# Superblocks of 480 columns in the second layer of an attention and two-layer MLP kernel

## The chip, the cores and the metric

The kernel runs on one core of a Trainium2 chip. The metric is the device time of one execution in microseconds: before the change 1749.05, the median of three runs between 1747.64 and 1750.35. The profile is one further execution with its own time.

## What is computed

Attention inside chunks of 64 tokens over q, k and v of shape (8, 8, 576, 64), and then two gated MLPs over the 4608 tokens, the second behind a normalization:

```python
attn_out = softmax(scale * q_c @ k_c.T) @ v_c          # by chunks of 64
x = attn_out.transpose(0, 2, 1, 3).reshape(4608, 512)
# first layer
g = x @ w_gate; h = g * sigmoid(g) * (x @ w_val)       # 512 -> 1536
x = h @ w_out                                          # 1536 -> 512
# second layer
xn = x / sqrt(mean(x * x) + 1e-6) * rms_g
g = xn @ w_gate2; h = g * sigmoid(g) * (xn @ w_val2)
out = h @ w_out2
```

All is float32. The kernel makes a product exact enough by splitting each operand into a high and a low part: one logical matmul is three on TensorE (`mm3`, lines 633 to 636).

## The kernel before

The tokens are cut into 36 tiles of 128. Eight of them are taken out of their order and put at the end: `last` (line 319), so that `home` says which tile stands at a position and `order` the reverse. A stretch of positions is therefore not always a stretch of rows of the output.

**First layer.** The first 28 positions make seven blocks of 512 tokens. They run as plain triple matmuls (`emit_g`, `emit_v`, `emit_y`), with the attention of later tiles, the conversion of the weights and the normalization of finished blocks spread between them on a list of positions. Each tile's attention result is split into `xh` and `xl` of its block, or, for the eight last tiles, stored to `x1_d` (`att_hi`, `att_lo`).

**Superblocks.** From line 1531 on the work goes by superblocks of two halves of equal width `tw` (`SB`, lines 904 to 909). Superblock 0 is the first layer for the eight last tiles (2 x 512 tokens); superblocks 1 to 5 are the second layer. A superblock uses a scheme of seven products in place of eight for 2 x 2 blocks. It has two stages:

- gate and value: for each of 6 chunks (`fp`) 14 products (7 for g, 7 for v, in the order of `GV`), each of 6 matmuls `tw` columns wide with one weight tile of 256 KB (`gv_mm`). After each one, `gv_after` takes the bank out on ScalarE (a copy, `snap`) and VectorE (sum, sigmoid, product).
- y: 42 items in pairs, in the order of `ORDER` for k and then `fp`, each of 2 x 3 matmuls (`y_mm`), fed by `h_prep`, which casts h on ScalarE and subtracts on VectorE, 8 items ahead. Behind the fifth of each six, `y_after` finishes a quarter. The output positions come in the order 11, 22, 21, 12 (the second digit is the half), after items 11, 29, 35 and 41; each is made of two pieces, q 0 and 1.

Weights stand in a ring of 16 tiles. `load_ring(wn + 16)` after each product, or each pair of items, issues the DMAs of those tiles whose place has come free, all on SP's queue. In the y stage the first tiles of the next superblock's gate products come in the same way, two behind each pair. SP issues in program order and waits at each instruction for what it needs.

**Output.** `y_out` adds and transposes a piece on VectorE into the tile `yo` (there are two, used in turn) and writes it with one DMA per 32 partitions and per run of contiguous output rows, `rows(t0 + j * tw, tw)`, on SP's queue (line 1180; in the last superblock some go on ScalarE's queue). In the last but one superblock the DMAs are held in a list, which `flush` issues during the last one. `x_load` and `x_prep` bring and split the next superblock's input in the y stage. In superblock 1 VectorE, ScalarE and GpSimd also run the normalization of the eight last tiles and the conversion of two chunks of weights, from the tables `late` and `norm`.

Of the kernel before, what the change touches and what calls it, by code (L numbers as in the profile page):

```python
# [19 lines left out]
def tile_kernel(  # L20
# [23 lines left out]
    P = 128  # L44
# [133 lines left out]
    def chunk(j, f):  # L178
        return f if j % 2 == 0 else NF - 1 - f
# [136 lines left out]

    NCH = NT // CH
    SC = S // CH
    last = [32, 33, 13, 34, 35, 21, 22, 23]
    home = [i for i in range(NT // P) if i not in last] + last  # L320
    order = [home.index(i) for i in range(NT // P)]

    def rows(t, n):
        runs = []
        for a in range(0, n, P):
            i = home[(t + a) // P]
            if runs and home[(t + a) // P - 1] == i - 1:
                runs[-1][1] += P
            else:
                runs.append([a, P, i * P])  # L330
        return runs

    EARLY = NW // P + 1
# [477 lines left out]
    def score_at(i):  # L811
        return NP + 7 * (i - 8)

    for i in range(NW // P, NT_):
        j = order[i] * P // NW
        if i >= 8:
            a = score_at(i)
# [66 lines left out]
    for j, p, nm in w1_at:  # L884
        a = 3 * min(chunk(j, 2 * p), chunk(j, 2 * p + 1)) + (3 if nm == "o" else 0)
# [17 lines left out]
    YTAG = {"g": {"A": "y2", "D": "a0", "C": "y0"}, "v": {"A": "y3", "D": "a1", "C": "y1"}}  # L903
    SB = [(TAIL, NW)]
    t0 = 0
    for tw in (512, 512, 512, 384, 384):
        SB.append((t0, tw))
        t0 += 2 * tw
    assert t0 == NT
# [245 lines left out]
    def y_out(s, q, pos, src, n):  # L1155
        nonlocal nout
        t0, tw = SB[s]
        m = "gv"[q]
        slow = s == len(SB) - 2 and pos != "11"
        if n:  # L1160
            tag = ("ysb0", "ysb1")[q] if slow and pos == "12" else ("acc", "sq")[nout % 2]
            shape = [P, 2, 512] if tag in ("ysb0", "ysb1") else [P, 512]
            t = st.tile(shape, F32, tag=tag, name=f"yt{q}{pos}_{s}")
            t = t[:, 0] if len(shape) == 3 else t
            nc.vector.tensor_add(t[:, :tw], src[:, :tw], snaps[m, n][:, :tw])
            src = t
        tag = ("acc", "sq")[nout % 2] if slow and pos == "21" else ("ah", "al")[nout % 2]
        o = st.tile([P, 512], F32, tag=tag, name=f"yo{q}{pos}_{s}")
        nout += 1
        nc.vector.transpose(out=o[:, :tw], in_=src[:, :tw])  # L1170
        i, j = int(pos[0]) - 1, int(pos[1]) - 1
        r0, c0 = t0 + j * tw, i * HK + q * P
        for a, (x, n, r) in [(a, run) for a in range(0, P, 32) for run in rows(r0, tw)]:
            dst = out[r:r + n, c0 + a:c0 + a + 32].rearrange("(b t) d -> t b d", t=32)
            src_ = o[a:a + 32, x:x + n].rearrange("t (b d) -> t b d", d=32)
            queue = nc.scalar if s == len(SB) - 1 and pos in ("12", "21") and a >= 64 else nc.sync
            if s == len(SB) - 2:
                held.append((dst, src_))
            else:
                queue.dma_start(out=dst, in_=src_)  # L1180
# [460 lines left out]
```

## Time and profile before

| | before |
|---|---|
| median of the runs | 1749.05 us |
| lowest, highest | 1747.64, 1750.35 us |
| profiled execution | 1741.64 us |
| its span | 1739.8 us |
| mean granted TensorE clock | 0.999 |
| TensorE busy | 1715.2 us, 99% |
| VectorE, ScalarE, GpSimd busy | 1271.6, 812.6, 543.9 us |

The span runs from the first to the last instruction. Times inside the trace are counted from its start. Matmul records overlap, since matmuls are pipelined; how fast they follow each other is read from their starts. "SPq" is SP's queue of DMA issues, DVE is VectorE, ACT ScalarE, POOL GpSimd, PE TensorE, PEld its weight loads. A bracket at the end of a timeline row is the idle time ahead of it and what ended that.

### The profile page before, as it was taken

The numbers are of one execution on the slowest core, as the hardware profiler recorded it, in microseconds if no ns is written. First come the engines' busy times: TensorE is split into PE (matmuls) and PEld (weight loads), VectorE is DVE, ScalarE is ACT, GpSimd is POOL, SyncE is SP. The second block draws the span as 40 slices with busy tenths as digits, with TensorE's granted clock in tenths as the row PEclk, the third lists the DMA queues.
The fourth block names the chain that finished last, engine by engine and source line by source line (L and its number), as shares of the span: only waits on it lengthen the run. The fifth ranks groups of instructions, "written<-read, shape, count | busy, mean of one in ns | idle before, by whom it ended". The sixth has DMA issues, their size and how long they took to land.

```text
span 1739.8 us, 29450 instructions
## 1 busy us (share of the span) xinstructions
PE 1715.2 (99%) x9978; PEld 1445.9 (83%) x9978; DVE 1271.6 (73%) x2232; ACT 812.6 (47%) x1902; POOL 543.9 (31%) x527
## 2 busy tenths in 40 slices
PE   7999999999999999999999999999999999999998
PEld 5788888888888888877877888888888888999998
DVE  6996777777678776467899678954885488569566
ACT  6773444445444444335556444532453354345343
POOL 1003546455555735334544632100210011002000
PEclk9999999999999999999999999999999999999999
DMA  9995878867786775856755797787678758989986
GB/s 233 332 248 147 229 199 218 238 172 211 216 209 209 194 228 192 289 166 226 243 173 176 224 317 233 207 257 217 180 206 266 211 170 245 301 267 273 285 253 175
DMA packets 462789, 392.86 MB, mean 226 GB/s; under 512 B 278832, under 2 KB 334896, under 8 KB 462640
## 3 DMA queue, kind: packets, MB, share of 16 engines
q1 hardware_dynamic: 423760, 311.68, 61.6%
q10 hardware_dynamic: 38880, 79.31, 14.4%
q8 instruction: 80, 1.31, 0.3%
q14 instruction: 69, 0.57, 0.1%
HBM read 310.90 MB, written 79.95 MB: 225 GB/s over the span
## 4 chain that ended last, share of the span: by engine, by line
PE 84%; DVE 7%; DMA 4%; ACT 2%; issue 1%; SPq 1%; POOL 0%; ACTq 0%; DVEq 0%; POOLq 0%
PE g L634 4%; PE g L635 4%; PE v L634 4%; PE g L636 4%; PE v L635 4%; PE v L636 4%; PE y L634 2%; PE y L635 2%; PE y L636 2%; PE y_b L635 2%; PE y_b L634 2%; PE y_b L636 2%; PE ygA L634 1%; PE ygA L635 1%; PE yvA L635 1%
## 5 line engine op out<-in xcount | busy, mean ns | idle before, releaser
L1094 POOL TENSOR_TENSOR h<-h,h 128x512 f32<-128x512 f32 (+1 forms) x36 | 46.6, 1294 | 506.0 <-DVE h L1072 499.6
L1130 DVE TENSOR_TENSOR hp<-h,hp 128x512 fp32r<-128x512 f32 (+1 forms) x216 | 147.4, 710 | 6.0 <-ACT hp L1129 5.9
L1052 ACT ACTIVATE sig<-sgt 128x512 f32<-128x512 f32 (+1 forms) x108 | 64.6, 598 | 186.8 <-DVE sgt L1060 186.7
L544 DVE STREAM_TRANSPOSE pT<-p 32x128 f32<-32x128 f32 x448 | 135.5, 303 | 17.9 <-POOL p L528 11.7
L1129 ACT CAST hp<-h 128x512 fp32r<-128x512 f32 (+1 forms) x216 | 121.3, 584 | 50.1 <-PE yvA L636 18.9
L1053 DVE TENSOR_TENSOR sgt<-sgt,sig 128x512 f32<-128x512 f32 (+1 forms) x108 | 77.0, 713 | 89.7 <-ACT sig L1052 89.7
L991 POOL TENSOR_TENSOR xf<-xf,xf 128x512 f32<-128x512 f32 (+1 forms) x48 | 81.7, 1702 | 170.8 <-DVE xo0l L987 75.0
L634 PE MATMUL g<-xh,wg 128*128 128x512 f32 x336 | 132.9, 395 | 2.1 <-ACT xh L608 1.1
L634 PE MATMUL v<-xh,wv 128*128 128x512 f32 x336 | 132.8, 395 | 1.7 <-DVE sg L663 1.0
L635 PE MATMUL g<-xl,wg 128*128 128x512 f32 x336 | 131.0, 390 | 0.4 <-DVE xl L628 0.4
L636 PE MATMUL g<-xh,l 128*128 128x512 f32 x336 | 131.0, 390 | 0.0
L636 PE MATMUL v<-xh,l 128*128 128x512 f32 x336 | 131.0, 390 | 0.0
L635 PE MATMUL v<-xl,wv 128*128 128x512 f32 x336 | 130.9, 390 | 0.0
L666 ACT CAST hh<-sg 128x512 fp32r<-128x512 f32 x84 | 52.1, 620 | 134.8 <-DVE sg L663 119.5
L646 ACT ACTIVATE sg<-g 128x512 f32<-128x512 f32 x84 | 50.1, 597 | 113.9 <-PE g L636 111.2
L528 POOL TENSOR_TENSOR p<-p,r 128x512 f32<-128x512 f32 x36 | 40.2, 1117 | 188.5 <-DVE r L527 131.7
L668 DVE TENSOR_TENSOR hl<-sg,hh 128x512 fp32r<-128x512 f32 x84 | 72.8, 866 | 35.2 <-ACT hh L666 34.5
L647 DVE SCALAR_TENSOR_TENSOR sg<-sg,g 128x512 f32<-128x512 f32 x84 | 57.3, 683 | 54.3 <-ACT sg L646 53.8
L1072 DVE TENSOR_TENSOR h<-h,sgt 128x512 f32<-128x512 f32 (+1 forms) x108 | 74.8, 693 | 3.7
L634 PEld LDWEIGHTS g<-xh,wg 128*128 128x128 f32 x336 | 63.0, 188 | 17.3 <-DVE sg L647 1.6
L634 PEld LDWEIGHTS v<-xh,wv 128*128 128x128 f32 x336 | 63.1, 188 | 16.4 <-DVE sg L663 2.0
L636 PEld LDWEIGHTS g<-xh,l 128*128 128x128 f32 x336 | 63.1, 188 | 13.7 <-DVE l L175 0.4
(855 smaller groups left out, 5254.4 us busy)
## 6 DMA issues: line engine op xcount, KB each, us to landing
wrg<-w_scratch SPq DMA_DIRECT2D x210, 256.0 KB, 3.5
wrv<-w_scratch SPq DMA_DIRECT2D x210, 256.0 KB, 3.5
wro<-w_scratch SPq DMA_DIRECT2D x210, 256.0 KB, 3.2
l<-lo_scratch ACTq DMA_DIRECT2D x51, 512.0 KB, 4.4
lo<-lo_scratch ACTq DMA_DIRECT2D x58, 256.0 KB, 4.8
w_scratch<-wsg ACTq DMA_DIRECT2D x18, 512.0 KB, 4.4
w_scratch<-wsv ACTq DMA_DIRECT2D x18, 512.0 KB, 4.1
xv<-in_v_dram SPq DMA_DIRECT2D x136, 64.0 KB, 4.3
```

Of the source, the lines that this page charges most:

```text
L544: nc.vector.transpose(out=pT[o:o + 32, :, r:r + 32], in_=pt[r:r + 32, :, z, b * 32:b * 32 + 32])
L634: nc.tensor.matmul(o, sh, mh, start=first, stop=False, skip_group_check=free)
L635: nc.tensor.matmul(o, sh, ml, start=False, stop=False, skip_group_check=free)
L636: nc.tensor.matmul(o, sl, mh, start=False, stop=last, skip_group_check=free)
L647: return sg, lambda: nc.vector.scalar_tensor_tensor(out=sg[:, :n], in0=sg[:, :n], scalar=1.0, in1=g[:, :n], op0=ALU.add, op1=ALU.mult)
L668: return product, lambda: nc.vector.tensor_sub(hl[:, :n], sg[:, :n], hh[:, :n].bitcast(F32))
L991: nc.gpsimd.tensor_sub(o, a, b)
L1052: nc.scalar.activation(sg[:, :tw], src[:, :tw], AF.Sigmoid)
L1053: nc.vector.tensor_mul(t[:, :tw], src[:, :tw], sg[:, :tw])
L1072: nc.vector.tensor_mul(h[:, :tw], src[:, :tw], sgt[pos][:, :tw])
L1129: nc.scalar.copy(hh[:, :tw], src)
L1130: nc.vector.tensor_sub(hl[:, :tw], src, hh[:, :tw].bitcast(F32))
```

## The change

The second layer's superblocks get the half widths 480, 480, 480, 480 and 384 in place of 512, 512, 512, 384 and 384. Their borders then no longer fall on tiles of 128 tokens, so `rows` works out the runs of output rows token by token: it walks to the end of a tile or of the stretch, whichever is nearer, and joins a piece to the run before it if the output rows follow on. The list of the eight tail tiles is changed: tile 16 takes the place of 13, and the order is 32, 33, 34, 35, 16, 21, 22, 23.

```diff
-    last = [32, 33, 13, 34, 35, 21, 22, 23]
+    last = [32, 33, 34, 35, 16, 21, 22, 23]
     home = [i for i in range(NT // P) if i not in last] + last
     order = [home.index(i) for i in range(NT // P)]
 
     def rows(t, n):
         runs = []
-        for a in range(0, n, P):
-            i = home[(t + a) // P]
-            if runs and home[(t + a) // P - 1] == i - 1:
-                runs[-1][1] += P
+        a = 0
+        while a < n:
+            i, p = home[(t + a) // P], (t + a) % P
+            step = min(P - p, n - a)
+            if runs and runs[-1][2] + runs[-1][1] == i * P + p:
+                runs[-1][1] += step
             else:
-                runs.append([a, P, i * P])
+                runs.append([a, step, i * P + p])
+            a += step
         return runs
...
     SB = [(TAIL, NW)]
     t0 = 0
-    for tw in (512, 512, 512, 384, 384):
+    for tw in (480, 480, 480, 480, 384):
         SB.append((t0, tw))
         t0 += 2 * tw
     assert t0 == NT
```

## Rows read from the trace of the kernel before

**Rows 1.** the page, part 1: busy time, share of the span, instructions of each engine

```profile
PE 1715.2 (99%) x9978; PEld 1445.9 (83%) x9978; DVE 1271.6 (73%) x2232; ACT 812.6 (47%) x1902; POOL 543.9 (31%) x527
```

**Rows 2.** superblocks 1 to 5: us, busy (x) PE PEld DVE ACT POOL, clock, DMA, GB/s

```profile
954.20:1127.60 173.40, 173.16 (x762) 142.39 (x761) 137.26 (x194) 82.75 (x150) 64.64 (x54) 1.00 0.78 247
1127.60:1299.20 171.60, 171.60 (x758) 141.82 (x757) 116.38 (x172) 70.25 (x122) 22.27 (x14) 1.00 0.72 214
1299.20:1471.10 171.90, 171.67 (x758) 141.84 (x757) 112.53 (x173) 68.32 (x122) 19.32 (x14) 1.00 0.75 220
1471.10:1603.00 131.90, 131.35 (x758) 130.98 (x757) 92.12 (x173) 56.74 (x122) 17.06 (x14) 1.00 0.89 280
1603.00:1733.80 130.80, 130.80 (x756) 130.80 (x755) 81.68 (x159) 51.60 (x108) 6.32 (x6) 1.00 0.82 245
```

**Rows 3.** timeline, TensorE: start, us, line, tiles; first and last matmuls of stages

```profile
1127.59 0.39 PE L634 MATMUL p0gA<-xo0h,wrg 128*128 128x512 f32 x1
...
1241.83 0.39 PE L634 MATMUL ygA<-hp,wro 128*128 128x512 f32 x1
...
1299.18 0.39 PE L634 MATMUL p0gA<-xo0h,wrg 128*128 128x512 f32 x1
...
1602.97 0.33 PE L634 MATMUL p0gA<-xo0h,wrg 128*128 128x384 f32 x1
...
1733.84 0.34 PE L636 MATMUL yvC<-hp,wro 128*128 128x384 f32 x1
```

**Rows 4.** timeline, TensorE, around product 14 of superblock 3

```profile
1317.99 0.39 PE L636 MATMUL p0vC<-xo6h,wrv 128*128 128x512 f32 x1
1318.61 0.47 PE L634 MATMUL p1gA<-xo0h,wrg 128*128 128x512 f32 x1 [0.23 <-DMA wrg<-w_scratch]
1318.92 0.39 PE L635 MATMUL p1gA<-xo0l,wrg 128*128 128x512 f32 x1
```

**Rows 5.** timeline, TensorE, stalls in superblocks 1 and 4

```profile
1014.31 0.50 PE L634 MATMUL p3vA<-xo0h,wrv 128*128 128x512 f32 x1 [0.24 <-DVE h L1072]
...
1578.04 0.44 PE L635 MATMUL ygC<-hp,wro 128*128 128x384 f32 x1 [0.55 <-DVE hp L1130]
```

**Rows 6.** timeline, SP's queue: issues of superblock 2's y stage and after, in order

```profile
1264.71 4.38 SPq L1180 DMA_DIRECT2D out_dram<-yo  x8
...
1274.65 6.88 SPq L928 DMA_DIRECT2D wro<-w_scratch  x10
...
1282.57 0.32 SPq L928 DMA_DIRECT2D wrv<-w_scratch  x1
1286.62 7.79 SPq L1180 DMA_DIRECT2D out_dram<-yo  x16
...
1297.39 6.03 SPq L1180 DMA_DIRECT2D out_dram<-yo  x8
...
1306.43 9.12 SPq L1180 DMA_DIRECT2D out_dram<-yo  x16
1315.65 0.41 SPq L928 DMA_DIRECT2D wrg<-w_scratch  x1
```

**Rows 7.** timeline, SP's queue: last two pieces of superblock 1

```profile
1125.13 4.17 SPq L1180 DMA_DIRECT2D out_dram<-yo  x8
...
1132.31 6.96 SPq L1180 DMA_DIRECT2D out_dram<-yo  x8
```

**Rows 8.** timeline, VectorE, at the start of superblock 3

```profile
1303.65 0.71 DVE L1170 STREAM_TRANSPOSE yo<-yt 128x512 f32<-128x512 f32 x1 [4.94 <-DMA out_dram<-yo]
```

**Rows 9.** stretches, early in the kernel (columns as in rows 2)

```profile
18.80:22.20 3.40, 3.40 (x72) 2.95 (x71) 2.94 (x7) 2.30 (x4) 1.92 (x2) 0.50 0.78 222
```

**Rows 10.** timeline, TensorE, just ahead of that stretch

```profile
15.74 0.69 PE L474 MATMUL s<-kT,qT 64*64 64x64 f32 x32 [1.52 <-ACT kT L440]
...
18.66 1.00 PE L552 MATMUL tp<-ident,p 128*128 128x128 f32 x4 [1.63 <-POOL p L528]
```

**Rows 11.** timeline, SP's queue: piece 22 of superblock 3

```profile
1456.43 4.17 SPq L1180 DMA_DIRECT2D out_dram<-yo  x8
```

## Prediction

> **What bounds the kernel now.** I read the page first: TensorE is busy in 99% of the span [rows 1]. The table of stretches, cut at the five superblocks of the second layer, says that this holds there too: 173.4, 171.6, 171.9, 131.9 and 130.8 us long, with TensorE busy for all but a few tenths of a microsecond in each, at full clock [rows 2]. VectorE (62 to 79% busy there) and the DMA engines (0.72 to 0.89) have room left on the average. So only two things can move the time: the pace of the matmuls, and stalls of TensorE. As every matmul record overlaps its neighbour, I take the pace from starts, not from durations.
>
> **Pace of the matmuls.** A superblock has 756 matmuls: 6 chunks x 14 products x 6, then 42 x 6, whatever its width. At 512 columns 504 of them start between 1127.59 and 1241.83 us: 114.24 / 504 = 226.67 ns each. At 384 columns the last superblock has 755 starts after its first between 1602.97 and 1733.84: 130.87 / 755 = 173.34 ns [rows 3]. The difference, 53.33 ns, is 128 columns at 2.4 GHz exactly; both are columns/2.4 + 13.3 ns. A matmul of 480 columns is not in the trace. Its bounds are its neighbours', 173.34 and 226.67; I take the line through both, 213.33 ns, because nothing but columns separates them. Then three superblocks at 226.67 and two at 173.34 make 1026.7 ns for one matmul of each, and four at 213.33 and one at 173.34 make 1026.7 too. The widths alone change nothing: 756 x 0. What is on VectorE, ScalarE and GpSimd keeps its number of operations and its columns and lies beside TensorE, as before.
>
> **Stalls that exist.** There is little to win. At the start of superblock 3 the first matmul of product 14 (p1gA) starts 0.62 us after the one before it where 0.23 is the pace, and the next one 0.08 late; the row names the DMA of its weight tile [rows 4]. That is 0.5 us. In the y stage the product ygC waits for VectorE's split of h, worst in superblock 4, where TensorE is idle for 0.55 us and the starts lose 0.8; by the same timeline it is about 0.2 in superblocks 1 and 2, none in 3 and 5. In the first superblock 0.5 us more is lost at p3vA, behind VectorE, which runs the tail's normalization in between [rows 5].
>
> **The runs of output rows.** Here the change adds something. An output piece goes out in 4 DMAs for each run of contiguous rows, for two quarters, so a position costs SP 8 issues per run. Before, only superblock 2 has a half with two runs (tiles 12 | 14, 15, 16), and the last one has one (13 | 34, 35). After: superblocks 1, 2 and 4 have one run in each half, superblock 3 has two in both (row tokens 1920 to 2047 | 2176 to 2527, and 2528 to 2687 | 3072 to 3391, since 16 and 21 to 23 are now missing from the order), the last one still two and one. Superblock 2 gives back 16 issues, superblock 3 gets 32 more.
>
> SP issues them in program order, and the ring's weight tiles stand behind them. Product 14 of the next superblock is the first whose weights are issued after the last output piece: 14 are already in the ring. Follow superblock 2 into 3 [rows 6], times against its end at 1299.18 [rows 3]: piece 22 (16 issues) from -12.56, in 7.79 us; six weight tiles, 2.9 to 3.0; piece 21 (8 issues) 6.03; six tiles; piece 12 (16 issues) 9.12; the weights of product 14 at +16.47. Its first matmul starts 2.96 us after the issue [rows 4, 6], at 19.43, where 14 products x 6 x 226.67 ns allow 19.04. This is the 0.4 us stall, and SP never waits for TensorE between 22 and 12. Superblock 1, with 8 issues everywhere, has ended piece 12 at 1139.3 (1132.31 + 6.96), +11.7 against its end at 1127.59 [rows 3, 7]: 4 us earlier than needed, with the 2.96.
>
> Small pieces cost SP as much as large ones: sixteen issues of half the mean size took 7.79 us, 0.49 each, when little else was queued. The Trainium skill (DMA: Bandwidth & Descriptors, Issuing engines are not separate DMA queues) calls the time to initiate a DMA "usually small relative to the DMA itself", and its section on the anatomy of a DMA gives about 50 ns of dispatch, for another path; by that, sixteen issues would be an estimated 0.8 us and superblock 3 would stall nothing. The rows speak against it for this queue.
>
> Now superblock 3 after the change, at 213.33 ns, against its end. Piece 22 can go out when VectorE has transposed it. Before, in superblock 2, that was 5.1 us after the quarter's last matmul (16.3 + 1.4 - 12.56); 15/16 of it is 4.8, so -15.36 - 1.28 + 4.8 = -11.8. Sixteen issues with their gap, 7.9: -3.9. Six tiles, 2.9: -1.0. Piece 21 now has 16 issues, behind six weight tiles as piece 12 was in superblock 2, so 9.2: +8.2. Six tiles, 2.9: 11.1. Piece 12, 9.2: 20.3. Issue to matmul, 2.96: 23.2. Allowed are 14 x 6 x 213.33 = 17.9. **Stall: 5.3 us.** Lower bound: both pieces at the quiet 7.9, which takes 2.6 off: 2.7. Upper: piece 11 has 16 issues as well, and the loads behind it (4 of x, then tiles at 0.69 us) may not be through at -11.8; they ended 3.7 us before piece 22 in superblock 2 [rows 6], piece 11 adds 3.5 (7.9 for 4.4), and the shorter pace takes 1 to 2 more: up to 1 us, 6.3. VectorE is also held longer: it is first in, first out, and piece 12's transposes waited 4.9 us for piece 21's DMAs to leave their tile [rows 8]. That hold will last until about +11 instead of +7, and the work behind it then reaches the banks of products 12 to 14 about as they are needed. It lies beside the SP stall, and adds nothing while that is the longer.
>
> **The clock.** TensorE has no such gap now. Near the start it did sparse small matmuls with gaps of 1.5 and 1.6 us, and the granted clock was 0.50 (1.2 GHz) in the following 3.4 us [rows 9, 10]. After a gap of 5 us the same can happen; a stretch of 3.4 us at half pace costs 1.7. Bounds 0 and 1.7; no row is of a single long gap, so I take the middle, 0.85.
>
> **Small terms.** The 0.5 us before superblock 3 go (its predecessor has 8 issues per piece now, and has 3 us to spare at 480: 11.8 + 3.0 against 17.9). The ygC stalls, one quarter of the way from 0.2 to 0.8, make 4 x 0.36 = 1.4 instead of 1.2: +0.2 (between -0.8 and +0.6). The first superblock's fixed work is pressed into 1/16 less time: +0.2 (0 to 0.8). Held pieces of the second last superblock keep 32 issues, which the last one's products still cover. Attention: tile 13 goes to block 3 and 16 to the tail, the same operations, both two blocks ahead of need: 0. The end: the last superblock keeps width, runs and queues: 0. Sum: 5.3 - 0.5 + 0.2 + 0.2 + 0.85 = **+6.0 us**. The profiled execution took 1741.6 us (span 1739.8) and would take 1747.6; it ran 7 us under the median of the runs, to which I add the same 6.0: **1755.0**.
>
> **Rivals.**
> (a) Not slower: VectorE reaches piece 22 earlier. Superblock 3 itself, with its 384-wide successor, had piece 22 out at 1456.43, 14.6 us ahead of its end at 1471.1 and so 3.1 us after the quarter's end instead of 5.1 [rows 2, 11]; it speaks against this that the successor is 480 wide now. With that and all pieces at 7.9 us, the tile goes out at 15.9 and arrives at 18.9: a stall of 0.9, and without a dip of the clock +0.8, 1749.9. It decides when product 14's tile is issued before +18.6, where the stall falls under 3.6.
> (b) SP's time in those issues is waiting on bytes, not on issues, and more pieces of the same bytes cost nothing. For it: eight large issues took between 4.2 and 7.0 us [rows 6, 7], so queued bytes do hold SP. Against it: sixteen took 7.79 for as many bytes as eight in 4.17. No stall then: -0.5 + 0.4, 1749.0. The Trainium skill's sentence above would have it so.
> (c) The matmul of 480 columns doesn't lie on the line. Rounded up to the price of 512 it costs 4 x 756 x 13.3 ns = 40 us, 1795; without the fixed 13.3 ns it gains 40, 1715. The exact 53.33 speaks against both. To be faster by 0.2% it would have to lie 3.1 ns under the line.
>
> **How the numbers follow.** 0.2% (3.5 us) is about what a measurement of this kernel tells from no change. Forecast 0.65, between 1751.3 (stall 2.7, nothing else) and 1758 (6.3 and every upper end); (a) 0.22; (b) 0.05; (c) 0.03 slower and 0.05 faster. The forecast's own low end is within 0.2%, the upper part of (a) with a clock dip is not: these balance. Slower 0.68, same 0.27, faster 0.05. Range 1748.5 to 1759.5: it holds the forecast, (b) by a little and most of (a), and leaves out (c) and the rest, under 2 in 10.
>
> **What would show it.** In the profile after: starts 213.3 ns apart at 480 columns; three rows of sixteen output issues on SP around the end of superblock 3, and one gap of TensorE of some 5 us at p1gA of superblock 4, released by the DMA of wrg; no such gap at superblock 3. A second stretch of half clock right behind it decides the clock term. Wrong it is if that gap is under 3 us, if another pace is seen, or if TensorE stalls at other superblocks' starts.

## The result, and the profile after

The changed kernel takes 1764.3 us (median of 5 runs, 1762.52 to 1766.7) where the kernel before takes 1748.06 (5 runs, 1747.49 to 1750.35): ratio 1.0088, 95% interval 1.0074 to 1.0102. It is slower by 16 us, as forecast in direction; the forecast was 6 us, and its range ended at 1759.5. The profiled execution of after took 1764.37 us, its span 1762.6.

The stretches of after, cut at the first matmul of each superblock of the second layer as those of before [rows 2] (columns: us, then busy time and count of PE, PEld, DVE, ACT, POOL, then the granted clock, the DMA share and GB/s), and a short one 24.7 us into superblock 4:

```profile
959.10:1124.60 165.50, 165.21 (x762) 142.39 (x761) 130.05 (x194) 79.36 (x150) 62.56 (x53) 1.00 0.81 257
1124.60:1288.40 163.80, 163.80 (x758) 141.90 (x757) 110.17 (x172) 66.61 (x122) 20.96 (x14) 1.00 0.77 227
1288.40:1454.00 165.60, 164.00 (x757) 141.79 (x756) 109.93 (x172) 66.61 (x122) 20.23 (x14) 1.00 0.73 217
1454.00:1624.90 170.90, 165.86 (x757) 142.99 (x757) 107.06 (x173) 65.36 (x122) 18.68 (x14) 0.99 0.78 230
1624.90:1755.80 130.90, 130.90 (x756) 130.87 (x756) 81.75 (x159) 51.68 (x108) 6.33 (x6) 1.00 0.82 241
1478.70:1482.00 3.30, 3.30 (x10) 2.75 (x9) 0.00 (x0) 0.56 (x1) 0.00 (x0) 0.50 0.98 349
```

Read it against a clean superblock. Superblock 2 has no idle time at all and takes 163.80 us, which is 756 matmuls at 216.67 ns. The line of the prediction gave 213.33. So the first thing to see is that even the undisturbed superblock is 2.5 us longer than forecast. Superblocks 3 and 4 add 1.8 and 7.1 us of their own; superblock 5 is what it was.

The sum from the starts of the matmuls: the five superblocks took 779.62 us before (954.2 to 1733.8) and take 796.75 now, 17.1 more. Work at pace, with 171.36 us for 756 matmuls at 512 columns and 131.05 at 384, was 3 x 171.36 + 2 x 131.05 = 776.2 and is 4 x 163.80 + 131.05 = 786.25: **10.1 us of pace**. What each superblock lost beyond it went from 2.0, 0.2, 0.5, 0.85 and 0 us to 1.7, 0, 1.8, 7.1 and 0: **7.0 us of stalls**. Together they are the 16.2 us between the medians, to within the spread of the runs. The profile of after also reaches superblock 1 some 5 us later than that of before (959.1 and 954.2); the experiment "The kernel before once more" shows that this is not the change.

The timeline of TensorE gives both (start, us, line, tiles; the bracket is the idle time before and what ended it):

```profile
1124.55 0.38 PE L637 MATMUL p0gA<-xo0h,wrg 128*128 128x480 f32 x1
...
1233.75 0.38 PE L637 MATMUL ygA<-hp,wro 128*128 128x480 f32 x1
...
1438.33 0.48 PE L637 MATMUL ygA<-hp,wro 128*128 128x480 f32 x1 [1.60 <-ACT s3g L1047]
...
1466.44 0.48 PE L637 MATMUL p0gA<-xo5h,wrg 128*128 128x480 f32 x1 [1.85 <-ACT s2g L1047]
...
1474.13 0.38 PE L639 MATMUL p0vC<-xo6h,wrv 128*128 128x480 f32 x1
1477.70 0.45 PE L637 MATMUL p1gA<-xo0h,wrg 128*128 128x480 f32 x1 [3.19 <-DMA wrg<-w_scratch]
...
1479.03 0.60 PE L639 MATMUL p1gA<-xo0h,wrg 128*128 128x480 f32 x1
1479.43 0.60 PE L637 MATMUL p1vA<-xo0h,wrv 128*128 128x480 f32 x1
```

The first two rows have 504 matmuls between them: 109.20 / 504 = 216.67 ns each, against 226.67 at 512 and 173.34 at 384 [rows 3]. The 3.19 us at p1gA is the forecast gap, behind the forecast DMA: product 14 (products are counted from 0) starts 23.67 us after superblock 4's start at 1454.03. Ahead of it TensorE is already idle for 1.85 us at p0gA, and for 1.60 in superblock 3 at ygA, which was not forecast. Counted by the starts, which come a little later still behind a gap, p1gA loses 3.4 us, p0gA 2.1 and ygA 1.8. From 1478.64 on matmuls start 0.40 us apart, 480 columns at 1.2 GHz, while the stretch above shows a clock of 0.50.

SP's queue around the end of superblock 3 (x16 is the number of issues in the row), which answers to [rows 6]:

```profile
1419.14 7.72 SPq L1183 DMA_DIRECT2D out_dram<-yo  x16
1426.96 2.79 SPq L931 DMA_DIRECT2D wro<-w_scratch  x6
1429.85 2.13 SPq L970 DMA_DIRECT2D xf<-xn_scratch  x4
...
1441.53 8.86 SPq L1183 DMA_DIRECT2D out_dram<-yo  x16
...
1454.37 8.17 SPq L1183 DMA_DIRECT2D out_dram<-yo  x16
...
1465.52 9.07 SPq L1183 DMA_DIRECT2D out_dram<-yo  x16
1474.69 0.40 SPq L931 DMA_DIRECT2D wrg<-w_scratch  x1
```

Four pieces (11, 22, 21, 12) of sixteen issues each. From 1441.53 to 1474.69 SP is issuing nearly all the time; the tile that product 14 wants goes out 20.66 us after the superblock's start (20.3 forecast), and its matmul starts 3.01 us later.

### The profile page after: what moved, and what is told of

The parts are those of the page before. It is cut to its first block, busy times and chain, and to the rows that moved or that the text cites. A ratio compares the mean times of both kernels' runs of the same rounds, so it can differ in the third digit from the quotient of the medians.

```text
span 1762.6 us, 29464 instructions
## 1 busy us (share of the span) xinstructions
PE 1727.8 (98%) x9978; PEld 1459.4 (83%) x9978; DVE 1271.6 (72%) x2232; ACT 813.5 (46%) x1902; POOL 543.0 (31%) x527
## 4 chain that ended last, share of the span: by engine, by line
PE 84%; DMA 5%; DVE 5%; SPq 2%; ACT 1%; issue 1%; POOL 1%; ACTq 0%; DVEq 0%; POOLq 0%
PE g L637 4%; PE g L638 4%; PE g L639 4%; PE v L637 4%; PE v L639 4%; PE v L638 4%; PE y L637 2%; PE y L639 2%; PE y L638 2%; PE y_b L637 2%; PE y_b L639 2%; PE y_b L638 2%; PE ygA L637 1%; PE ygA L639 1%; PE ygA L638 1%; PE yvA L638 1%
## 5 line engine op out<-in xcount | busy, mean ns | idle before, releaser
L1097 POOL TENSOR_TENSOR h<-h,h 128x480 f32<-128x480 f32 (+2 forms) x36 | 46.6, 1295 | 524.0 <-DVE h L1075 517.6
L1055 ACT ACTIVATE sig<-sgt 128x480 f32<-128x480 f32 (+2 forms) x108 | 64.5, 598 | 189.9 <-DVE sgt L1063 189.7
L1133 DVE TENSOR_TENSOR hp<-h,hp 128x480 fp32r<-128x480 f32 (+2 forms) x216 | 146.1, 703 | 6.2 <-ACT hp L1132 6.1
L547 DVE STREAM_TRANSPOSE pT<-p 32x128 f32<-32x128 f32 x448 | 135.6, 303 | 16.3 <-POOL p L531 10.0
L1132 ACT CAST hp<-h 128x480 fp32r<-128x480 f32 (+2 forms) x216 | 121.4, 584 | 50.0 <-PE yvA L639 23.3
L1056 DVE TENSOR_TENSOR sgt<-sgt,sig 128x480 f32<-128x480 f32 (+2 forms) x108 | 76.9, 712 | 90.4 <-ACT sig L1055 90.4
L994 POOL TENSOR_TENSOR xf<-xf,xf 128x480 f32<-128x480 f32 (+2 forms) x48 | 81.0, 1687 | 172.1 <-DVE xo0l L990 122.4
L1075 DVE TENSOR_TENSOR h<-h,sgt 128x480 f32<-128x480 f32 (+2 forms) x108 | 74.4, 689 | 3.7
L666 DVE SCALAR_TENSOR_TENSOR sg<-v,sg 128x512 f32<-128x512 f32 x84 | 57.6, 686 | 26.0 <-PE v L639 24.8
```

The source lines that it names most:

```text
L547: nc.vector.transpose(out=pT[o:o + 32, :, r:r + 32], in_=pt[r:r + 32, :, z, b * 32:b * 32 + 32])
L666: nc.vector.scalar_tensor_tensor(out=sg[:, :n], in0=vv[:, :n], scalar=0.5, in1=sg[:, :n], op0=ALU.mult, op1=ALU.mult)
L994: nc.gpsimd.tensor_sub(o, a, b)
L1055: nc.scalar.activation(sg[:, :tw], src[:, :tw], AF.Sigmoid)
L1056: nc.vector.tensor_mul(t[:, :tw], src[:, :tw], sg[:, :tw])
L1075: nc.vector.tensor_mul(h[:, :tw], src[:, :tw], sgt[pos][:, :tw])
```

## The experiments

**Widths put back, order and runs alone.** The changed kernel with the old widths.

```
-    for tw in (480, 480, 480, 480, 384):
+    for tw in (512, 512, 512, 384, 384):
```

> The new tail order and the new rows, with the old widths 512, 512, 512, 384, 384. Theory: of the 16 us, about 10 come from the pace of the 480-column matmuls and 8 to 9 from the stalls around superblock 3 and 4 that its 64 output issues make; the order and the rows alone cost nothing. Here all halves of superblocks 1 to 4 are one run, so also the 0.5 us stall at superblock 3 goes: 1747 to 1749 us, ratio 0.999 to 1.001. Rival: the order of the tail tiles itself disturbs the first layer (the gap of 4.0 us at the ssq matmul and its half-clock stretch): then 5 us over the kernel before, ratio 1.003.

Measured: 1747.43 us (10 runs) against 1747.39 (13 runs), ratio 0.9998 (0.9989 to 1.0008). With these widths each half of superblocks 1 to 4 is one run. The gap at product 14 of superblock 3 [rows 4] is gone:

```profile
1304.64 0.39 PE L637 MATMUL p0gA<-xo0h,wrg 128*128 128x512 f32 x1
...
1323.45 0.39 PE L639 MATMUL p0vC<-xo6h,wrv 128*128 128x512 f32 x1
1323.68 0.39 PE L637 MATMUL p1gA<-xo0h,wrg 128*128 128x512 f32 x1
...
1476.00 0.33 PE L637 MATMUL p0gA<-xo0h,wrg 128*128 128x384 f32 x1
```

Product 14 starts 0.23 us after its predecessor, and the superblock takes 171.36 us, exactly the pace. So other tail tiles and the new way to work out the runs cost nothing, and the half microsecond that they win is too small to be measured. The whole loss comes with the widths.

**Five widths in one kernel.** The same line, to read the pace of each width.

```
+    for tw in (512, 480, 448, 448, 416):
```

> Half widths 512, 480, 448, 448, 416: a look at the pace of each width in the stretches without a stall. Theory A (on the line columns/2.4 + 13.3 ns where the width is a multiple of 64 columns, 3.3 ns above it otherwise): 226.7, 216.7, 200.0, 200.0, 190.0 ns. Theory B (the same with multiples of 128): 448 columns take 203.3 ns too. Theory C (13/12 of columns/2.4, with 512 the exception): 448 take 202.2 and 416 take 187.8 ns. Rival: the excess has nothing to do with the width but with what else runs then: 448 and 416 lie anywhere between 198 and 206 and between 185 and 193, and the single starts scatter.

Measured from starts: 512 columns 226.75 ns, 480 216.66 (755 starts), 448 202.67 (612 starts from 1297.55 to 1421.58, and 202.66 in the next superblock), 416 188.34 (755 starts). One run took 1767.41 us.

```profile
1133.75 0.38 PE L637 MATMUL p0gA<-xo0h,wrg 128*128 128x480 f32 x1
...
1297.33 0.38 PE L639 MATMUL yvC<-hp,wro 128*128 128x480 f32 x1
1297.55 0.36 PE L637 MATMUL p0gA<-xo0h,wrg 128*128 128x448 f32 x1
...
1421.58 0.36 PE L637 MATMUL ygC<-hp,wro 128*128 128x448 f32 x1
```

The 216.7 ns belong to the width of 480, wherever the superblock stands and whatever its runs are. Over columns / 2.4 GHz the four widths stand 13.4, 16.7, 16.0 and 15.0 ns. None of the three rules of the expectation (200.0, 203.3 or 202.2 at 448; 190.0, 190.0 or 187.8 at 416) gives all of them. Against the rival, that the excess comes from what else runs, stand the two superblocks at 448: they agree to 0.01 ns.

**The old tail tiles with the new widths.** This moves issues from superblock 3 to superblock 2: both then have 48.

```
-    last = [32, 33, 34, 35, 16, 21, 22, 23]
+    last = [32, 33, 13, 34, 35, 21, 22, 23]
```

> Widths 480, 480, 480, 480, 384 and new rows, with the old order of the tail tiles. Superblocks 2 and 3 then have one half of one run and one of two: 48 issues each in place of 32 and 64. Theory: the pace stays at 216.7 ns (10.1 us); each of the two boundaries behind them stalls at p1gA by 1 to 2 us, without a half-clock stretch and without the gaps at ygA and p0gA: 5 to 6 us less than the changed kernel, 1758 to 1760 us, ratio 1.006. Rival (the stalls come from the width and not from the number of issues): the gaps at ygA, p0gA and p1gA of 2.0, 2.2 and 3.6 us stay, 1764 us.

Measured: 1759.62 us (4 runs), ratio 1.0066 (1.0049 to 1.0083). The gaps moved with the issues; there is now one at product 14 of superblock 3 and one of superblock 4, a little larger than expected, none at ygA or p0gA, and no half clock:

```profile
1310.92 0.45 PE L637 MATMUL p1gA<-xo0h,wrg 128*128 128x480 f32 x1 [2.61 <-DMA wrg<-w_scratch]
...
1476.64 0.45 PE L637 MATMUL p1gA<-xo0h,wrg 128*128 128x480 f32 x1 [1.67 <-DMA wrg<-w_scratch]
```

**Half of superblock 3's output DMAs left out.** Its pieces then have 8 issues each, as before the change, and half its output columns are not written.

```
         for a, (x, n, r) in [...]:
+            if s == 3 and a >= 64:
+                continue
```

> The changed kernel, with superblock 3 leaving out half of its output DMAs (the 32-partition groups 64 and 96), so that it issues 32 and not 64; half of its output columns are not written. Theory: SP's chain is 8 x 0.49 us shorter per piece position; the gaps at ygA, p0gA and p1gA and the half-clock stretch go, 8 to 9 us: 1755 to 1757 us, ratio 1.004 to 1.005. What stays is the pace, 10 us. Rival (VectorE's and ScalarE's work at 480 columns makes the gaps): they stay, 1764 us.

Measured: 1755.49 us (4 runs), ratio 1.0045 (1.003 to 1.006): 8.8 us less than after, which is what superblocks 3 and 4 lost beyond their pace (1.8 + 7.1). Both now take 163.80 us. SP's pieces and product 14 of superblock 4:

```profile
1419.25 3.78 SPq L1185 DMA_DIRECT2D out_dram<-yo  x8
...
1439.96 3.95 SPq L1185 DMA_DIRECT2D out_dram<-yo  x8
...
1449.53 4.30 SPq L1185 DMA_DIRECT2D out_dram<-yo  x8
...
1456.80 4.96 SPq L1185 DMA_DIRECT2D out_dram<-yo  x8
```

```profile
1470.26 0.38 PE L639 MATMUL p0vC<-xo6h,wrv 128*128 128x480 f32 x1
1470.47 0.38 PE L637 MATMUL p1gA<-xo0h,wrg 128*128 128x480 f32 x1
```

What stays, 8.1 us, is the pace (10.1) less the small stalls that are gone (about 2). The run takes away bytes with the issues, so it doesn't tell them apart; the next one does.

**The kernel before, with superblock 1's runs cut in two.** Same bytes, same rows, 512 columns; only the number of issues of superblock 1 doubles, to 64.

```
+    def split2(runs):
+        return [h for a, n, r in runs for h in ([a, P, r], [a + P, n - P, r + P])]
...
-        for a, (x, n, r) in [(a, run) for a in range(0, P, 32) for run in rows(r0, tw)]:
+        for a, (x, n, r) in [(a, run) for a in range(0, P, 32) for run in (split2(rows(r0, tw)) if s == 1 else rows(r0, tw))]:
```

> The kernel before (widths 512), with the output runs of superblock 1 cut in two by hand, so that it issues 64 DMAs and not 32; the same bytes go to the same rows. The pace of the matmuls is untouched. Theory (SP's issues at 0.49 us each hold the weights behind them): with the sum of the prediction at 226.67 ns, piece 22 at -12.6 and then 7.9, 2.9, 9.2, 2.9, 9.2 and 2.96 us, the matmul of product 14 comes at +22.5 where 19.0 are allowed: gaps of 3.4 us in all at p0gA and p1gA of superblock 2, with or without a half-clock stretch (up to 1.7): 1750.5 to 1753 us, ratio 1.002 to 1.003. Rival (more pieces of the same bytes cost SP nothing, and the gaps need 480 columns): 1747.5 us, ratio 1.000.

Measured: 1757.02 us (4 runs) against 1748.3, ratio 1.0044 (1.0029 to 1.0059); more than expected. SP's issues, and product 14:

```profile
1121.28 9.61 SPq L1183 DMA_DIRECT2D out_dram<-yo  x16
...
1133.87 9.11 SPq L1183 DMA_DIRECT2D out_dram<-yo  x16
...
1145.96 9.64 SPq L1183 DMA_DIRECT2D out_dram<-yo  x16
```

```profile
1158.78 0.76 PE L637 MATMUL p1gA<-xo0h,wrg 128*128 128x512 f32 x1 [3.26 <-DMA wrg<-w_scratch]
```

In the kernel before the last two of these pieces were issued in 4.17 and 6.96 us [rows 7]. Product 14 starts 23.58 us after the superblock's start at 1135.20, with the gap at the same matmul as in after. So more issues of the same bytes are enough to make the gap, without the width of 480 and without the new tail. The 8.7 us are, by the starts, 1.3 at ygA, 1.1 at p0gA, 3.4 at p1gA, about 1.4 for half clock (0.50 from 1158.3 to 1161.6), and 1.5 more at the product 14 of superblock 3 (its first matmul was 0.4 and 0.6 us late in two profiles of the kernel before, 2.1 here). Superblock 2, whose issues delay that product, has no more of them than before; whether its longer gap comes from the cut or from this execution is not shown.

**The pace at eighteen widths.** In the kernel before, four of the seven products (k = 4, 5, 2 and 6) of g and of v in each superblock stream only part of their columns, and the rest of those products is not computed; the one with k = 6 uses 64 stationary columns instead of 128 in superblocks 1 and 3.

```
+    SWEEP = {1: {4: (32, 480, P), 5: (0, 480, P), 2: (64, 448, P), 6: (0, 480, 64)}, ...}
...
+        a, n, q = SWEEP.get(s, {}).get(k, (0, tw, P))
-            c = slice(kt * P, (kt + 1) * P)
+            c = slice(kt * P, kt * P + q)
-                o, w[:, 0, c], w[:, 1, c], xh[:, kt, :tw], xl[:, kt, :tw],
+                o[:q, a:a + n], w[:, 0, c], w[:, 1, c], xh[:, kt, a:a + n], xl[:, kt, a:a + n],
```

> The kernel before, where the gate and value products k = 4, 5, 2 and 6 of each superblock stream only a part of the columns (the rest of those products is not computed): 464, 448, 432, 416 in superblock 2; 496, 504, 400 in 3; 368 to 320 in 4; 304 to 256 in 5; in superblock 1 columns 32 to 511 and 0 to 479 and 64 to 511; and 480 and 512 columns with a stationary operand of 64 columns. A look at the pace of each. Theory (the width decides, and only multiples of 128 columns come as cheap as columns/2.4 + 13.3 ns): 480 takes 216.7 wherever it begins; 448 takes 203.3, 416 188.3; 496, 464 and 432 lie 15 to 17 ns over columns/2.4; 256 takes 120 ns unless the weight loads hold it at some 173. Rival A (the place of the first column decides): 480 from column 32 takes another time than from 0. Rival B (the weight load decides): with 64 stationary columns 480 comes down to the line, 213.3, or lower, and 512 too.

Measured, as the mean distance of some 66 starts inside runs of twelve equal matmuls (ns), and what of it is over columns / 2.4. Single distances more than some 12% above the middle one are left out as stalls: twelve at 272 columns, four at 256 (119.98 ns with them), two at 480 with 64 stationary columns:

| columns | pace | over | columns | pace | over | columns | pace | over |
|---|---|---|---|---|---|---|---|---|
| 512 | 226.67 | 13.3 | 416 | 188.73 | 15.4 | 320 | 146.55 | 13.2 |
| 504 | 226.91 | 16.9 | 400 | 181.05 | 14.4 | 304 | 137.68 | 11.0 |
| 496 | 220.0 | 13.3 | 384 | 173.36 | 13.3 | 288 | 131.67 | 11.7 |
| 480 | 216.36 | 16.4 | 368 | 166.74 | 13.4 | 272 | 125.26 | 11.9 |
| 464 | 209.64 | 16.3 | 352 | 160.55 | 13.9 | 256 | 119.0 | 12.3 |
| 448 | 202.36 | 15.7 | 336 | 153.74 | 13.7 | | | |
| 432 | 196.18 | 16.2 | | | | | | |

With 64 stationary columns 480 took 219.36 and 512 took 230.3, not less, though each weight load took 0.13 to 0.14 us in place of 0.19. A start at column 32 or 64 didn't help either (218.03 at 480 in the disturbed superblock 1, 202.27 at 448). So 480 is on the upper side of a band of 11 to 17 ns, and both anchors of my line, 512 and 384, happened to lie at 13.3. That only multiples of 128 are cheap is refuted (496, 320 to 368). The length of the weight load is not it either. What sets the step is left open.

**The kernel before once more.** No edit; this is to see whether the first layer changed.

> The kernel before, one more profile. The profile of the changed kernel has a gap of 4.0 us at the first-layer matmul ssq (block 1) and a half-clock stretch behind it, 5 us in all, ahead of everything that the change touches; the profiled execution of the kernel before has not, and is itself 4 us faster than any timed run of it. Theory: the gap belongs to most executions of either kernel: block 1 takes 109 to 112 us here too (106.4 in the profile of before), and the whole 1745 to 1749. Rival: it comes with the change: block 1 takes 106.4 us again.

Measured: 1749.41 us, span 1747.6. After shows an idle gap of 4 us in the first layer that the first profile of before doesn't have. The second one has it too, behind the same engine. The matmul ssq in the first profile of before, in this one, and in after:

```profile
190.40 0.50 PE L742 MATMUL ssq<-ah,ones 128*128 128x512 f32 x1 [0.15 <-ACT p L500]
```

```profile
194.90 0.80 PE L742 MATMUL ssq<-ah,ones 128*128 128x512 f32 x1 [3.88 <-ACT p L500]
```

```profile
193.63 0.80 PE L745 MATMUL ssq<-ah,ones 128*128 128x512 f32 x1 [3.99 <-ACT p L503]
```

and in this run the clock behind it:

```profile
193.30:200.00 6.70, 5.10 (x12) 4.05 (x13) 4.71 (x12) 6.06 (x18) 3.60 (x5) 0.50 0.73 173
```

That block takes 111.7 us in both this run and after, 106.4 in the first profile. The gap stands in every other profile of this document too, of either kernel, with 3.4 to 4.0 us. So it is no effect of the change: the profile that the prediction was made from, 1741.64 us, was of the one execution without this stall, 4 us under the fastest timed run of the kernel before (1745.79). In superblocks 1 to 5, after minus this run is 17.0 us, as with the first profile.

**Half of two pieces on ScalarE's queue.** In after, pieces 21 and 12 of superblock 3 issue half their DMAs on ScalarE, as the last superblock does.

```
-            queue = nc.scalar if s == len(SB) - 1 and pos in ("12", "21") and a >= 64 else nc.sync
+            queue = nc.scalar if s in (3, len(SB) - 1) and pos in ("12", "21") and a >= 64 else nc.sync
```

> The changed kernel, with half of the DMAs of superblock 3's pieces 21 and 12 (partition groups 64 and 96) issued on ScalarE's queue, as in the last superblock. Theory: SP issues 8 and 8 there in place of 16 and 16, so product 14's weights come 7 to 8 us earlier; the gap at p1gA (3.6 us) and the half-clock stretch (1.6) go, that at p0gA (2.2) shrinks: 1757 to 1760 us, ratio 1.006. The gap at ygA (2.0), which lies ahead of these pieces, stays. Rival (ScalarE, which then waits for the transposes in its own queue, delays its copies of the banks by as much): 1762 to 1766 us.

Measured: 1769.05 us (4 runs), ratio 1.011 (1.0092 to 1.0129), 5 us worse than after. The gap at p1gA is gone, but a larger one stands ahead of it:

```profile
1471.83 0.77 PE L637 MATMUL p0gA<-xo4h,wrg 128*128 128x480 f32 x1 [7.80 <-ACT s1g L1047]
```

```profile
1453.14 5.87 ACTq L1183 DMA_DIRECT2D out_dram<-yo  x8
...
1465.24 5.93 ACTq L1183 DMA_DIRECT2D out_dram<-yo  x8
1471.21 0.56 ACT L1047 COPY s1g<-p0gA 128x480 f32<-128x480 f32 x1 [11.57 <-DMA out_dram<-yo]
```

The rival of the expectation came out, worse than its number. ScalarE empties the PSUM banks that the next products need; its copy of p0gA came 11.6 us after the instruction before it, 5.6 of them until the second piece's first issue and 5.9 in its issues. The gap at ygA stayed, as expected (2.2 us idle).

**The load of x ahead of piece 11.** In after, the load of superblock 4's x that stood behind piece 11's sixteen issues is moved ahead of them.

```
+                if n == 10 and s == 3:
+                    x_load(s + 1, 1)
+                    xnext = x_prep(s + 1, 1)
...
-                if n == 16 and s + 1 < len(SB):
+                if n == 16 and s + 1 < len(SB) and s != 3:
```

> The changed kernel, with the second half of superblock 4's input (four DMAs, x_load) put on SP's queue before piece 11 of superblock 3 and not 6 items after it. A look. Theory for the gap at ygA (2.0 us): the loads stand behind the 16 issues of piece 11, land late, and ScalarE waits 2.8 us for them with its copy of the bank (s3g) behind the waiting cast. Then the gap at ygA is under 0.3 us here, and the gaps at p0gA and p1gA stay at 5 to 6 us in all. Rival: the gap comes from VectorE's work at 480 columns (the split of h ahead of it): it stays at 1.8 to 2.0 us.

Measured: 1764.07 us (one run). The gap at ygA is gone and superblock 3 takes 163.80 us. In after the cast of x waited for its DMA and the copy that frees ygA's bank stood behind it on ScalarE; here the same cast waits for nothing. After, then this kernel:

```profile
1435.20 0.59 ACT L989 CAST xo0h<-xf 128x480 fp32r<-128x480 f32 x1 [2.79 <-DMA xf<-xn_scratch]
...
1437.72 0.55 ACT L1047 COPY s3g<-ygA 128x480 f32<-128x480 f32 x1
```

```profile
1434.87 0.59 ACT L989 CAST xo0h<-xf 128x480 fp32r<-128x480 f32 x1
```

So this is the cause of the ygA gap. At p0gA and product 14 the starts still lose 1.5 and 3.2 us, 4.7 in all where 5 to 6 were expected. Superblocks 3 and 4 together take 333.9 us, 336.6 in after; the whole is no lower because this execution came to superblock 1 2.5 us later (961.57 and 959.06), and one run can't tell 2.7 us.

**Piece 12 in tiles of its own.** In after, VectorE no longer waits for piece 21's DMAs before it transposes piece 12 of superblock 3.

```
+        if s == 3 and pos == "12":
+            o = st.tile([P, 2, 512], F32, tag=f"ysb{q}", name=f"yo{q}{pos}_{s}")[:, 0]
+        else:
             o = st.tile([P, 512], F32, tag=tag, name=f"yo{q}{pos}_{s}")
```

> The changed kernel, with piece 12 of superblock 3 transposed into two tiles of its own, so that VectorE doesn't wait for piece 21's DMAs to leave theirs (6.6 and 2.6 us in the changed kernel). A look. Theory, as in the prediction: the wait of VectorE makes the gap at p0gA (2.1 us) but lies beside SP's chain, which sets the end: the gap at p0gA goes, that at p1gA grows from 3.4 to 5 or 5.6 us, and the time from the start of superblock 4 to the matmul of product 14 stays 23.2 to 23.7 us. Rival: the two are in a row: p1gA keeps its 3.4 us, and product 14 comes 2.1 us earlier, at 21.6.

Measured: 1764.49 us (one run). In after VectorE's transposes of piece 12 wait 6.6 and 2.6 us for the DMAs of the tile:

```profile
1460.24 0.68 DVE L1173 STREAM_TRANSPOSE yo<-yt 128x480 f32<-128x480 f32 x1 [6.61 <-DMA out_dram<-yo]
...
1464.09 0.68 DVE L1173 STREAM_TRANSPOSE yo<-yt 128x480 f32<-128x480 f32 x1 [2.62 <-DMA out_dram<-yo]
```

Without that hold the gap at p0gA is gone, but the gap at product 14 stays at 3.1 us by the starts, where 5 to 5.6 were expected:

```profile
1478.75 0.74 PE L637 MATMUL p1gA<-xo0h,wrg 128*128 128x480 f32 x1 [2.96 <-DMA wrg<-w_scratch]
```

Product 14 is at +21.3 against the superblock's start. By these two numbers the rival (3.4 and 21.6) came out. But the reason is another: superblock 3 took 2.0 us longer here (167.7 us, 165.7 in after; its gap at ygA was 2.05 us idle, with half clock behind it), and so the start that +21.3 is counted from came later. SP's queue tells more. It issues nearly all the time from piece 22 to the tile that product 14 wants, here for 32.3 us and in after for 33.2:

```profile
1443.40 8.13 SPq L1186 DMA_DIRECT2D out_dram<-yo  x16
...
1454.50 9.60 SPq L1186 DMA_DIRECT2D out_dram<-yo  x16
...
1467.08 8.56 SPq L1186 DMA_DIRECT2D out_dram<-yo  x16
1475.74 0.40 SPq L931 DMA_DIRECT2D wrg<-w_scratch  x1
```

From piece 11's first issue to product 14 it takes 58.2 us (1420.53 to 1478.75) where after takes 58.6, and superblocks 3 and 4 together take 336.1 us, 336.6 in after. So SP's issues set the end, and VectorE's hold lies beside them, as the prediction had it.

## Why the prediction was right or wrong

- **Pace of the matmuls: the step that failed.** Its bounds (173.34 and 226.67) held, the value chosen between them did not: 480 columns take 216.67 ns and not 213.33. That is 3.33 ns x 3024 = 10.1 us, where "756 x 0" stood. "Nothing but columns separates them" was an inference from two points, and two points always lie on a line; the sweep shows a band of 11 to 17 ns in which both points happened to sit at 13.3. A slope of exactly 1 / 2.4 GHz was no evidence for the widths between. Rival (c) named this mechanism, but only with its far ends (40 us either way) and a chance of 0.03 for the slower one; an intermediate price, a few ns over the line, had no place in range or chances. "Another pace is seen" was among the prediction's own signs of being wrong. What makes 480 columns dearer than the line stays open. The Trainium skill (TensorE: Matmul & The Clock Gate, "Wait — 56ns, not 53.3ns?") gives columns / 2.4 GHz plus about 2.5 ns for back-to-back matmuls, an estimated 202.5 ns at 480; the trace has 216.67, and no width of the sweep comes near that sum (11.0 ns over columns / 2.4 GHz at the least).
- **Stalls that exist: right.** The half microsecond at product 14 of superblock 3 went, in after and in the kernel with order and rows alone.
- **The runs of output rows: right in mechanism and size.** Product 14 was forecast at +23.2 us and a stall of 5.3; it came at +23.67, with 3.4 + 2.1 = 5.5 us lost. The chain is that of the prediction: 0.5 to 0.6 us per issue, sixteen issues a piece, the ring's tiles behind them. That the sum fits so closely is in part luck: piece 22 went out at -12.5 and not -11.8 us and took 9.0 and not 7.9, the six tiles behind it 3.9 and not 2.9, piece 21 8.3 and not 9.2, and the allowed time was 18.2 and not 17.9. The split of runs in the kernel before shows it alone, the half set of issues takes it away. Rival (b), bytes and not issues, falls with the first of these: same bytes, and the gap is there. Rival (a) falls with the issue of product 14's tile at +20.66, where it wanted one before +18.6. That a part of the stall shows ahead of p1gA came from VectorE's hold, which the prediction placed at products 12 to 14 and which stood at product 8 (p0gA); without the hold that gap went and product 14 came no sooner.
- **Left out: piece 11.** The prediction counted piece 11's sixteen issues only for what they delay at piece 22. The four loads of x right behind them come late as well, and through ScalarE they cost 1.8 us at ygA. The load ahead of the piece shows this. The prediction followed the weights in SP's queue to their consumer, and not the loads.
- **The clock: right in kind, low in size.** One stretch of 0.50 behind the gap cost about 1.5 us; the sum had 0.85, the middle of 0 and 1.7.
- **Small terms.** The ygC stalls were to cost 0.2 and went away in superblocks 2 and 4, -1.1. The first superblock's were to cost 0.2 and came out at -0.3.

The sum as measured, in the profiles: 10.1 + 5.5 + 1.8 + 1.5 - 0.5 - 1.1 - 0.3 = 17.0, against +6.0 forecast; 10.1 of the missing 11 are the pace. The base was sound: the profile of before ran 7 us under the median, and the forecast added its terms to the median.

## What to carry to other kernels

A stream's cost at a size that the trace does not show is not known from a line through two sizes that it does show: price the size by its own run, or let the range hold a few ns either way, multiplied by the count (3 ns, 3024 times, are 9 us here). Where output is cut into more DMAs, count issues and not bytes, and follow everything in the same queue, loads as well as weights, to the first consumer that needs it. A queue on another engine is no free relief when that engine also frees PSUM banks.

## What the hardware showed

- The pace of these matmuls over columns / 2.4 GHz is not constant: 13.3 ns at 512, 496 and 384 columns, 16 to 17 at 504, 480, 464 and 432, 11 to 12 at 256 to 304. At 480 single distances alternate between 212 or 213 and 220 or 221 ns in the kernel with five widths; in superblock 2 of after all lie between 215 and 218, with the same mean of 216.67. At half clock it is columns / 1.2 GHz: 400 ns at 480 (after), 427 at 512 (the kernel with the runs cut in two).
- One idle gap of 3.2 us was followed by 3.3 us at a clock of 0.50, in two kernels and at the same matmul (p1gA of superblock 4 in after, of superblock 2 in the kernel with the runs cut in two). Around the gap of 3.9 us in the first layer the clock was 0.50 for 6.7 us. The gaps of 2.6 and 1.7 us in the kernel with the old tail were followed by none, but gaps of 2.2 and 2.05 us at ygA were (in the runs with half of two pieces on ScalarE's queue and with piece 12 in tiles of its own; the starts behind them are 400 ns apart). So the length of a gap alone did not decide it here.
- In superblocks 1 to 3 eight output DMAs held SP's queue for 3.8 us (half of superblock 3's output left out) to 7.3 us (piece 12 of superblock 2 in after), and sixteen for 7.7 (after) to 10.3 us (the kernel with the old tail): 0.47 to 0.91 us each. SP's waits are in these times, so the price of an issue alone is not shown by them.
